# Decays of two chunks built by TensorE in PSUM ahead of block 0 of a fused SSD scan and MLP, and chunk 1's scan moved to the end of block 0

## Chip, cores, metric

One core of one Trainium2 chip. The metric is the time of one execution on the device in microseconds (us), the median of several runs; lower is better. The span of a profile is some 1.7 us shorter than the time of the same run (411.6 against 413.28 for the kernel before).

## The reference

A Mamba-2 style scan over 4 batches, 8 heads, 768 steps in chunks, then an MLP with hard-swish. Cut to what matters:

```python
log_a = np.log(np.clip(a, 1e-06, 1.0))          # a: (4, 8, 768)
for c in range(nc):
    cum = np.cumsum(la, axis=-1)
    L = np.exp(cum[:, :, :, None] - cum[:, :, None, :]) * causal     # the decays
    M = np.einsum('bhin,bhjn->bhij', Cc, Bc) * L
    y[:, :, sl] = M @ xc + (Cc @ state) * np.exp(cum)
    state = exp(sum(la)) * state + sum(B x * exp(cum[-1] - cum))
x = y.transpose(0, 2, 1, 3).reshape(3072, 256)
h = x @ w_in;  g = h * np.clip(h + 3.0, 0.0, 6.0) / 6.0;  out = g @ w_out   # w_in, w_out in float64
```

The kernel works on chunks of 128 steps. All 4 batches of one chunk (512 tokens) form one block of the MLP, so there are six blocks. The weights come as 64-bit floats and are decoded on the chip in eight parts, four of w_in and four of w_out, while block 0 runs.

## The kernel before

The decays of a chunk come by DMA: the cumulative sum is written to DRAM and read back, spread over all 128 partitions. GpSimd masks the upper triangle, and ScalarE takes the exp of one head at a time, with minus the sum at step j as its bias.

```python
nc.sync.dma_start(out=cum_d.rearrange("c g p -> g c p"), in_=cum)

def load_decay(c, b):
    L = big([P, NH, P], "L")
    src = cum_d[c, b * NH:(b + 1) * NH].rearrange("h p -> (h p)").unsqueeze(0)
    nc.sync.dma_start(out=L.rearrange("j h i -> j (h i)"), in_=src.to_broadcast([P, NH * P]))
    Ls[c, b] = L

def hide(c, b):                       # GpSimd, 128x1024
    nc.gpsimd.affine_select(out=L, in_=L, pattern=[[0, NH], [1, P]], compare_op=ALU.is_ge,
                            fill=-1e5, base=0, channel_multiplier=-1)
def decay(c, b):                      # ScalarE, 128x128 each
    for h in range(NH):
        nc.scalar.activation(L[:, h], L[:, h], AF.Exp, bias=cum_n[:, c, g:g + 1])
```

`turn` transposes B and C of two batches on TensorE, `scores` forms C B' of one batch on TensorE and multiplies it into L on VectorE, `mix` multiplies by x on TensorE, `keep` copies y and the state out. A decode of one weight part goes back and forth between ScalarE and VectorE:

```python
def decode(i):                                     # five stages, one per `yield`
    nc.scalar.copy(out=s, in_=top); yield
    e = s & 0x7FF0; s = s & 0x8000; yield          # VectorE
    nc.scalar.activation(e..., AF.Relu, ...); nc.scalar.activation(e, ..., AF.Relu, ...)
    m = hi & 0xFFFFF | 0x100000; yield             # VectorE
    m = lo * 2**-32 + m; e = e | s; load_w(i + NRAW); yield
    dst = m * 2**-20 * e                           # VectorE, writes w_in or w_out
```

The order of block 0, cut: the prologue runs chunk 0's scan; the first half (`mlp_in`) has chunk 1's exps and transposes between its columns; the second half (`mlp_out`) has chunk 1's scan beside the first batches.

```python
for f in range(NF):
    mlp_in(0, f); ...decode stages...; beside_in(1, f)    # exps, turn of chunk 1
beside_out(1, 0)
for i in range(NP):
    for b in range(2):
        mlp_out(0, b, i * FP, (i + 1) * FP)               # needs w_out part i
    ...decode stages of w_out...
    beside_out(1, i + 1)                                  # scores, mix, keep of chunk 1
mlp_out(0, 2, 0, NF); beside_out(1, 4); mlp_out(0, 3, 0, NF)
```

## Time and profile before

| | before |
|---|---|
| time, median (range) of 3 runs | 411.64 us (410.7 to 414.11) |
| block 0's first product h (end of the prologue) | 31.4 us |
| last part of w_in and first of w_out ready (end of the first half) | 67.7 us |
| block 1's first product h (end of the second half) | 112.2 us |
| from there to the end of the span | 299.4 us |

Read it as four stages: the first three are limited by different things, and the last is TensorE without a hole. The prediction shows the lines for this.

### The profile page before, as it was taken

How to read it: one execution, taken by the hardware profiler on the slowest of the kernel's cores; microseconds unless marked ns; L12 is line 12 of the kernel's file. 1: busy time of each engine (PE TensorE's matmuls, PEld its weight loads, DVE VectorE, ACT ScalarE, POOL GpSimd, SP SyncE). 2: the span in 40 equal slices, each digit the busy share in tenths (PEclk: the TensorE clock that was granted, in tenths of full speed). 3: DMA queues.
4: the chain of work that ended last, by engine and by line, in shares of the span. 5: the costliest groups of instructions: out<-in, count | busy, mean ns of one | idle time of the engine just before them, and what ended most of it. 6: DMA issues, size and time to landing. Idle time of an engine off the chain costs nothing.

```text
span 411.6 us, 6492 instructions
## 1 busy us (share of the span) xinstructions
PE 378.7 (92%) x2588; PEld 261.3 (63%) x2588; DVE 227.3 (55%) x414; ACT 163.0 (40%) x365; POOL 40.4 (10%) x42
## 2 busy tenths in 40 slices
PE   0487798759999999999999999999999999999995
PEld 0353344548844698844698844698744789744995
DVE  5367787990448864138854238844238834257611
ACT  5386899520179300079200188200188200133100
POOL 1326100060006000005000004000000000000000
PEclk9999989998999999999999999999999999999999
DMA  9897966940096000097000096000000000000000
GB/s 158 236 337 245 150 249 128 161 146 25 14 118 229 2 1 27 3 119 237 0 2 27 21 125 216 0 2 27 27 0 0 2 2 28 26 0 0 2 27 25
DMA packets 87614, 32.33 MB, mean 79 GB/s; under 512 B 75584, under 2 KB 81408, under 8 KB 87584
## 3 DMA queue, kind: packets, MB, share of 16 engines
q1 hardware_dynamic: 87584, 31.92, 37.3%
q8 instruction: 20, 0.33, 0.3%
q14 instruction: 10, 0.08, 0.1%
HBM read 28.67 MB, written 3.24 MB: 78 GB/s over the span
## 4 chain that ended last, share of the span: by engine, by line
PE 74%; DMA 9%; ACT 5%; issue 4%; DVE 4%; SPq 1%; POOL 1%; POOLq 0%; DVEq 0%; ACTq 0%
PE h L377 29%; PE ob L450 18%; PE oa L450 13%; PE o L391 6%; DMA L<-cum_d 5%; ACT L L250 3%; PE cb L304 3%; DMA bc<-in_C_dram 2%; PE y L336 2%; PE y L327 1%; DVE gT L383 1%; DMA eto<-cum_d 1%; ACT r L382 1%; POOL L L241 1%; SPq L202 1%
## 5 line engine op out<-in xcount | busy, mean ns | idle before, releaser
L377 PE MATMUL h<-yT,w_in 128*128 128x512 f32 x384 | 169.9, 598 | 4.7 <-DVE w_in L181 3.8
L377 PEld LDWEIGHTS h<-yT,w_in 128*128 128x128 f32 x384 | 72.2, 192 | 91.1 <-issue 78.8
L383 DVE SCALAR_TENSOR_TENSOR gT<-r,h 128x512 f32<-128x512 f32 x96 | 64.3, 683 | 61.6 <-ACT r L382 61.2
L382 ACT ACTIVATE r<-h,half 128x512 f32<-128x512 f32 x96 | 64.5, 685 | 73.4 <-PE h L377 70.3
L250 ACT ACTIVATE L<-L,cum_n 128x128 f32<-128x128 f32 x192 | 58.4, 397 | 4.5 <-POOL L L241 4.5
L312 DVE TENSOR_TENSOR L<-L,cb 128x256 f32<-128x256 f32 x96 | 33.8, 414 | 28.6 <-PE cb L304 28.6
L450 PE MATMUL ob<-t,gT 128*128 128x128 f32 x320 | 39.8, 278 | 0.0
L359 ACT COPY yT<-y 128x256 f32<-128x256 f32 x24 | 7.7, 374 | 80.5 <-PE y L344 61.7
L450 PEld LDWEIGHTS oa<-w_out,gT 128*128 128x128 f32 x320 | 37.2, 192 | 3.7 <-issue 3.7
L450 PEld LDWEIGHTS ob<-t,gT 128*128 128x128 f32 x320 | 37.3, 192 | 2.7 <-issue 2.7
L241 POOL TENSOR_SCALAR_AFFINE_SELECT L<-L 128x1024 f32<-128x1024 f32 x24 | 31.2, 1309 | 78.7 <-DMA L<-cum_d 67.6
L450 PE MATMUL oa<-w_out,gT 128*128 128x128 f32 x320 | 38.4, 276 | 0.0
L450 PE MATMUL ob<-w_out,s 128*128 128x128 f32 x320 | 38.2, 278 | 0.0
L450 PEld LDWEIGHTS ob<-w_out,s 128*128 128x128 f32 x320 | 36.5, 192 | 1.8 <-issue 1.5
L391 PE MATMUL o<-w_out,gT 128*128 128x256 f32 x128 | 30.6, 399 | 6.7 <-DVE w_out L181 6.7
L391 PEld LDWEIGHTS o<-w_out,gT 128*128 128x128 f32 x128 | 25.1, 199 | 11.8 <-DVE w_out L181 7.5
L304 PE MATMUL cb<-cT,bT 32*128 32x256 f32 x192 | 22.6, 472 | 6.5 <-DVE cT L285 5.4
L481 DVE TENSOR_TENSOR u<-ob,res 128x256 f32<-128x256 f32 x10 | 4.2, 425 | 30.6 <-PE ob L450 30.6
L450 PE MATMUL oa<-t,s 128*128 128x128 f32 x160 | 19.5, 275 | 0.0
L450 PEld LDWEIGHTS oa<-t,s 128*128 128x128 f32 x160 | 18.7, 192 | 0.0
L304 PEld LDWEIGHTS cb<-cT,bT 32*128 32x128 f32 x192 | 10.5, 203 | 12.6 <-DVE cT L285 6.5
L471 DVE TENSOR_TENSOR res<-oa,x 128x256 f32<-128x256 f32 x10 | 4.2, 425 | 24.4 <-PE oa L450 15.8
(64 smaller groups left out, 248.8 us busy)
## 6 DMA issues: line engine op xcount, KB each, us to landing
L<-cum_d SPq DMA_DIRECT2D x24, 512.0 KB, 6.9
raw<-in_moe_w_in_dram SPq DMA_DIRECT2D x4, 1024.0 KB, 8.3
raw<-in_moe_w_out_dram SPq DMA_DIRECT2D x4, 1024.0 KB, 6.8
xt<-in_x_dram SPq DMA_DIRECT2D x6, 512.0 KB, 8.7
out_dram<-res SPq DMA_DIRECT2D x20, 128.0 KB, 1.8
bc<-in_C_dram SPq DMA_DIRECT2D x6, 256.0 KB, 5.1
bc<-in_B_dram SPq DMA_DIRECT2D x6, 256.0 KB, 7.6
eto<-cum_d SPq DMA_DIRECT2D x40, 32.0 KB, 5.9
```

The lines of the kernel that those rows point to most:

```text
L241: nc.gpsimd.affine_select(out=L, in_=L, pattern=[[0, NH], [1, P]], compare_op=ALU.is_ge, fill=-1e5, base=0, channel_multiplier=-1)
L250: nc.scalar.activation(L[:, h], L[:, h], AF.Exp, bias=cum_n[:, c, g:g + 1])
L304: nc.tensor.matmul(out=cb.rearrange("j h i -> j (h i)"), lhsT=bT[rows, b % 2], rhs=cT[rows, b % 2].rearrange("n t i -> n (t i)"), start=Tr ...
L312: nc.vector.tensor_tensor(out=L[:, hs], in0=L[:, hs], in1=cbs[q], op=ALU.mult)
L336: nc.tensor.matmul(out=y_ps[u][32 * q:32 * q + 32, b % 2], lhsT=xt[:, b * NH + h], rhs=L[:, h], start=(c == 0), stop=True, tile_position=( ...
L359: nc.scalar.copy(out=yTs[c][:, u, bs_], in_=y_ps[u][:, 0:2])
L377: nc.tensor.matmul(out=h, lhsT=w_in[:, j, f * P:(f + 1) * P], rhs=yTs[k][:, j].rearrange("p b i -> p (b i)"), start=(j == 0), stop=(j == N ...
L382: nc.scalar.activation(r, h, AF.Relu, bias=half, scale=1.0 / 6.0)
L383: nc.vector.scalar_tensor_tensor(out=gTs[k][:, f], in0=r, scalar=1.0, in1=h, op0=ALU.min, op1=ALU.mult)
L391: nc.tensor.matmul(out=o, lhsT=gTs[k][:, f, b * P:(b + 1) * P], rhs=w_out[:, f], start=(f == 0), stop=(f == NF - 1))
L450: nc.tensor.matmul(out=bank[:, slot], lhsT=lhs[:, j], rhs=rhs[:, j], start=(j == 0), stop=(j == NJ - 1), skip_group_check=True)
L471: nc.vector.tensor_tensor(out=res[:, 0:5:4], in0=oa[:, 1:3], in1=x1[:, t:t + 1].to_broadcast([P, 2, P]), op=ALU.add)
```

## The change

Intent: spare chunks 0 and 1 the trip of their decays through DRAM, and take chunk 1's scan away from the weight decode. The differences cum_i - cum_j come from a product with 64 rows of contraction (32 rows carry cum_i, 32 carry -cum_j, and selecting vectors pick the batch and the head), added in PSUM onto a mask of 0 and -1e5 that a bf16 product with the identity has put there. ScalarE then takes the exp of 128x512 at once. All of it lies ahead of block 0. Chunk 1's scan moves to the last two batches of block 0's second half. The core of the diff, with cuts:

```diff
+    def diff_mask(c, b, u):
+        nc.tensor.matmul(
+            out=d, lhsT=ident_h, rhs=hide.unsqueeze(1).to_broadcast([P, HU, P]),
+            start=True, stop=True)
+    def diff_add(c, b, u):                       # 64 rows of contraction
+        nc.tensor.matmul(
+            out=ds[c, b, u], lhsT=d_lhs[:, b], rhs=d_rhs[:, HU * u:HU * u + HU],
+            start=False, stop=True, skip_group_check=True)
+    def diff_exp(c, b, u):
+        nc.scalar.activation(Ls[c, b][:, HU * u:HU * u + HU], ds.pop((c, b, u)), AF.Exp)
 ...
-    for b in range(NB):
-        hide(0, b)
+    for b in range(NB):
+        for u in range(2):
+            diff_mask(0, b, u)
+    ... log, scan, spread ...
+    for b in range(NB):
+        for u in range(2):
+            diff_add(0, b, u)
 ...
     scores(0, 0)
     scores(0, 1)
+    diff(1, 0, 0)                # mask, add, exp
+    diff(1, 0, 1)
     mix(0, (0,))
+    diff(1, 1, 0)
     scores(0, 2)
+    diff(1, 1, 1)
     mix(0, (1,))
 ...  (four more of chunk 1 among the rest)
         if k == 0:
-            beside_out(c, 0)
             for i in range(NP):
                 ... mlp_out(0, b, i * FP, (i + 1) * FP), decode of w_out ...
-                    beside_out(c, i + 1)
-            mlp_out(k, 2, 0, NF)
-            beside_out(c, 4)
+                if i + 2 == NP:
+                    ... from_start(1), carry(1), ends(1, b), turn(1, 0), turn(1, 1)
+            beside_out(1, 0)
+            mlp_out(0, 2, 0, NF // 2)
+            beside_out(1, 1)
+            ... and so on to beside_out(1, 4)
```

Smaller parts: `ends` uses the last column of L and not a separate exp; chunk 0's x is loaded earlier; one of four weight sums moves.

More of the change, by code (lines that the diff above doesn't have):

```diff
@@ L14 @@
 ALU = mybir.AluOpType
+AX = mybir.AxisListType
 PSUM = bass.MemoryType.PSUM
@@ L67 @@
     ctx.enter_context(tc.manual_schedule())
-    def big(shape, name):
-        return att.tile(shape, FP32, name=name, tag="big", bufs=8)
+    pre = ffn.tile([P, NF, TB], FP32, name="pre", tag="gT")
+    G = NB * NH
     moe_w_in, moe_w_out = moe_w_in.bitcast(U32), moe_w_out.bitcast(U32)
-    a_sb = big([NB * NH, S], "a_sb")
-    nc.sync.dma_start(out=a_sb, in_=a.rearrange("b h s -> (b h) s"))
+    a_sb = pre[:2 * G, 0:2].rearrange("g t i -> g (t i)")[:, :S]
+    for r in range(2):
+        nc.sync.dma_start(out=a_sb[r * G:(r + 1) * G], in_=a.rearrange("b h s -> (b h) s"))
     loaded = {}
@@ L115 @@
     load_bc(0)
+    load_x(0)
     nc.scalar.preload_act_table_set("natural_log_exp_and_others")
@@ L120 @@
     make_identity(nc, ident)
-    run = big([NB * NH, NC, P], "run")
+    ident_h = const.tile([P, P], BF16, name="ident_h")
+    hide = const.tile([P, P], BF16, name="hide")
+    nc.gpsimd.memset(hide, 0.0)
+    nc.gpsimd.affine_select(
+        out=hide, in_=hide, pattern=[[1, P]], compare_op=ALU.is_ge, fill=-1e5, base=0,
+        channel_multiplier=-1)
+    run = pre[:2 * G, 2:4].rearrange("g t i -> g (t i)")[:, :S]
+    run = run.rearrange("g (c p) -> g c p", p=P)
     nc.vector.memset(run, 1.0)
     nc.vector.memset(run[:, :, 0:1], 0.0)
+    nc.vector.tensor_copy(ident_h, ident)
     half = const.tile([P, 1], FP32, name="half")
@@ L139 @@
     nc.vector.tensor_reduce(
-        out=parity, in_=head.rearrange("p q t -> p t q"), axis=mybir.AxisListType.X,
+        out=parity, in_=head.rearrange("p q t -> p t q"), axis=AX.X,
         op=ALU.add)
@@ L182, in decode @@
             out=dst, in0=m, scalar=2.0 ** -20, in1=e, op0=ALU.mult, op1=ALU.mult)
-    cum = big([NB * NH, NC, P], "cum")
-    rest = big([NB * NH, NC, P], "rest")
-    flat = cum.rearrange("g c p -> g (c p)")
-    nc.vector.tensor_scalar(
-        out=a_sb, in0=a_sb, scalar1=1e-6, scalar2=1.0, op0=ALU.max, op1=ALU.min)
-    nc.scalar.activation(a_sb, a_sb, AF.Ln)
-    nc.vector.tensor_tensor_scan(
-        out=flat, data0=run.rearrange("g c p -> g (c p)"), data1=a_sb, initial=0.0,
-        op0=ALU.mult, op1=ALU.add)
@@ L194 @@
-    cum_d = dram.tile([NC, NB * NH, P], FP32, name="cum_d")
-    nc.sync.dma_start(out=cum_d.rearrange("c g p -> g c p"), in_=cum)
+    one_h = const.tile([2 * G, NH], FP32, name="one_h")
+    one_b = const.tile([2 * G, NB], FP32, name="one_b")
+    eye = ident[:2 * G, :2 * G]
+    nc.vector.tensor_reduce(
+        out=one_h, in_=eye.rearrange("g (x h) -> g h x", h=NH), axis=AX.X, op=ALU.add)
+    nc.vector.tensor_reduce(
+        out=one_b, in_=eye.rearrange("g (r b h) -> g b r h", r=2, h=NH), axis=AX.XY, op=ALU.add)
@@ new lines @@
+    nc.vector.tensor_scalar(
+        out=one_b[G:], in0=one_b[G:], scalar1=-1.0, scalar2=None, op0=ALU.mult)
+    d_lhs = pre[:2 * G, 6].rearrange("g (b j) -> g b j", b=NB)
+    d_rhs = pre[:2 * G, 7:9].rearrange("g t (h i) -> g (t h) i", i=P)
+    nc.vector.tensor_copy(d_lhs[:G], one_b[:G].unsqueeze(2).to_broadcast([G, NB, P]))
+    nc.gpsimd.tensor_copy(d_rhs[G:], one_h[G:].unsqueeze(2).to_broadcast([G, NH, P]))
+    cum = pre[:2 * G, 4:6].rearrange("g t i -> g (t i)")[:, :S]
+    cum_c = cum.rearrange("g (c p) -> g c p", p=P)
@@ new lines, with log_a, add_up, spread @@
+    ends_at = (slice(0, P), slice(P, S))
+    def log_a(sl):
+        nc.vector.tensor_scalar(
+            out=a_sb[:, sl], in0=a_sb[:, sl], scalar1=1e-6, scalar2=1.0, op0=ALU.max, op1=ALU.min)
+        nc.scalar.activation(a_sb[:, sl], a_sb[:, sl], AF.Ln)
+    def add_up(sl):
+        nc.vector.tensor_tensor_scan(
+            out=cum[:, sl], data0=run.rearrange("g c p -> g (c p)")[:, sl], data1=a_sb[:, sl],
+            initial=0.0, op0=ALU.mult, op1=ALU.add)
+    def spread(engine, c):
+        engine.tensor_tensor(
+            out=d_lhs[G:], in0=cum_c[G:, c:c + 1].to_broadcast([G, NB, P]),
+            in1=one_b[G:].unsqueeze(2).to_broadcast([G, NB, P]), op=ALU.mult)
+        for u in range(2):
+            hs = slice(HU * u, HU * u + HU)
+            engine.tensor_tensor(
+                out=d_rhs[:G, hs], in0=cum_c[:G, c:c + 1].to_broadcast([G, HU, P]),
+                in1=one_h[:G, hs].unsqueeze(2).to_broadcast([G, HU, P]), op=ALU.mult)
@@ L197 @@
+    cum_d = dram.tile([NC, G, P], FP32, name="cum_d")
     Ls, etos = {}, {}
     def load_decay(c, b):
-        L = big([P, NH, P], "L")
+        Ls[c, b] = L = att.tile([P, NH, P], FP32, name="L", bufs=2 * NB)
         src = cum_d[c, b * NH:(b + 1) * NH].rearrange("h p -> (h p)").unsqueeze(0)
@@ L203, in load_decay @@
             out=L.rearrange("j h i -> j (h i)"), in_=src.to_broadcast([P, NH * P]))
-        Ls[c, b] = L
     def load_eto(c):
@@ L212, in load_eto, with conceal @@
         etos[c] = eto
-    for b in range(NB):
-        load_decay(0, b)
-    load_x(0)
-    load_w(1)
-    load_w(2)
-    cum_n = const.tile([P, NC, NB * NH], FP32, name="cum_n")
-    e_from = const.tile([P, NC, NB * NH], FP32, name="e_from")
-    def by_token():
-        nc.vector.tensor_tensor(
-            out=rest, in0=cum[:, :, P - 1:P].to_broadcast([NB * NH, NC, P]), in1=cum,
-            op=ALU.subtract)
-        c_ps = ps.tile([P, 2, NC, NB * NH], FP32, name="c_ps", tag="f")
-        for k, src in enumerate((cum, rest)):
-            for c in range(NC):
-                nc.tensor.transpose(
-                    out=c_ps[:, k, c], in_=src[:, c], identity=ident[:NB * NH, :NB * NH])
+    cum_n = const.tile([P, NC, G], FP32, name="cum_n")
+    def by_token():
+        c_ps = ps_o.tile([P, NC, G], FP32, name="c_ps", tag="o")
+        for c in range(2, NC):
+            nc.tensor.transpose(out=c_ps[:, c], in_=cum_c[:G, c], identity=ident[:G, :G])
         nc.vector.tensor_scalar(
-            out=cum_n, in0=c_ps[:, 0], scalar1=-1.0, scalar2=None, op0=ALU.mult)
-        nc.scalar.activation(e_from, c_ps[:, 1], AF.Exp)
+            out=cum_n[:, 2:], in0=c_ps[:, 2:], scalar1=-1.0, scalar2=None, op0=ALU.mult)
     yTs, states, bTs, bss, tmps, y_pss, CBs = {}, {}, {}, {}, {}, {}, {}
-    def hide(c, b):
+    ds = {}
+    def diff_mask(c, b, u):
+        k = 2 * b + u
+        if c == 0 and k < 4:
+            d = ps.tile([P, HU, P], FP32, name="d", tag="f")
+        elif c == 0 and k >= 6:
+            d = ps_y.tile([P, HU, P], FP32, name="d", tag=f"y{u}")
+        else:
+            d = ps_o.tile([P, HU, P], FP32, name="d", tag="o")
+        nc.tensor.matmul(
+            out=d, lhsT=ident_h, rhs=hide.unsqueeze(1).to_broadcast([P, HU, P]),
+            start=True, stop=True)
+        ds[c, b, u] = d
+    def diff_add(c, b, u):
[3 more added lines that the diff above has]
+    def diff_exp(c, b, u):
+        if u == 0:
+            Ls[c, b] = att.tile([P, NH, P], FP32, name="L", bufs=2 * NB)
+        nc.scalar.activation(Ls[c, b][:, HU * u:HU * u + HU], ds.pop((c, b, u)), AF.Exp)
+    def conceal(c, b):
         L = Ls[c, b]
@@ L253, in from_start, with ends, carry @@
         nc.scalar.activation(etos[c], etos[c], AF.Exp)
-    def ends(c):
-        bc, xt = loaded[c]
+    def ends(c, b):
         if c < NC - 1:
-            bs = att.tile([P, NB * NH, N], FP32, name="bs")
+            if b == 0:
+                bss[c] = att.tile([P, G, N], FP32, name="bs")
+            hs = slice(b * NH, b * NH + NH)
             nc.gpsimd.tensor_tensor(
-                out=bs, in0=bc[:, 1],
-                in1=e_from[:, c].unsqueeze(2).to_broadcast([P, NB * NH, N]), op=ALU.mult)
-            bss[c] = bs
-        if 0 < c < NC - 1:
-            tmp = att.tile([P, NB, 2 * D], FP32, name="tmp", bufs=1)
+                out=bss[c][:, hs], in0=loaded[c][0][:, 1, hs],
+                in1=Ls[c, b][:, :, P - 1:P].to_broadcast([P, NH, N]), op=ALU.mult)
+    def carry(c):
+        if c < NC - 1:
+            tmps[c] = att.tile([P, NB, 2 * D], FP32, name="tmp", bufs=1)
             nc.gpsimd.tensor_tensor(
-                out=tmp, in0=states[c - 1],
+                out=tmps[c], in0=states[c - 1],
                 in1=etos[c][:, :, P - 1:P].to_broadcast([P, NB, 2 * D]), op=ALU.mult)
-            tmps[c] = tmp
     def turn(c, p):
         bc, xt = loaded[c]
-        t_ps = ps_o.tile([P, 4, P], FP32, name="t_ps", tag="o")
+        pool, tag = (ps, "f") if c < 2 else (ps_o, "o")
+        t_ps = pool.tile([P, 4, P], FP32, name="t_ps", tag=tag)
         for k in range(4):
@@ L299, in scores @@
             rows = slice(32 * q, 32 * q + 32)
-            if c == 0 and b % 2 and q < 2:
-                cb = ps_o.tile([P, 2, P], FP32, name="cb", tag="o")
-            else:
-                cb = ps.tile([P, 2, P], FP32, name="cb", tag="f")
+            cb = ps.tile([P, 2, P], FP32, name="cb", tag="f")
             nc.tensor.matmul(
@@ L318, in mix @@
         if bs[0] % 2 == 0:
-            y_pss[c] = [ps_y.tile([P, 4, P], FP32, name=f"y{u}") for u in range(NK)]
+            y_pss[c] = [ps_y.tile([P, 4, P], FP32, name=f"y{u}", tag=f"y{u}") for u in range(NK)]
         y_ps = y_pss[c]
@@ L411, in weight_sums @@
         t2, t4 = (att.tile([P, NJ, P], FP32, name=n, tag="wm") for n in ("t2", "t4"))
-        for o, p_, q_, op in ((t3, w4[:, 1, 1], w4[:, 0, 1], ALU.subtract),
+        t1 = w4[:, 0, 1]
+        wsums.update({1: t1, 2: t2, 3: t3, 4: t4})
+        for o, p_, q_, op in ((t3, w4[:, 1, 1], t1, ALU.subtract),
                               (t2, t3, w4[:, 0, 0], ALU.add),
-                              (t4, w4[:, 1, 0], t2, ALU.subtract)):
+                              (t4, w4[:, 1, 0], t2, ALU.subtract),
+                              (t1, t1, w4[:, 0, 0], ALU.subtract)):
             nc.vector.tensor_tensor(out=o, in0=p_, in1=q_, op=op)
-        wsums.update({1: w4[:, 0, 1], 2: t2, 3: t3, 4: t4})
-    def weight_sum_in_place():
-        nc.vector.tensor_tensor(
-            out=w4[:, 0, 1], in0=w4[:, 0, 1], in1=w4[:, 0, 0], op=ALU.subtract)
+            yield
     gsums = {}
@@ L492, in beside_in, with rows @@
     def beside_in(c, f):
-        if c > 1 and f < 2:
-            hide(c, 2 * f)
-            hide(c, 2 * f + 1)
+        if f < 2:
+            conceal(c, 2 * f)
+            conceal(c, 2 * f + 1)
         if f == 3:
             from_start(c)
-        if f == 4:
-            ends(c)
-        if f in ((4, 8, 12, 15) if c == 1 else (2, 4, 6, 8)):
-            decay(c, (f - 1) // 4 if c == 1 else f // 2 - 1)
+            carry(c)
+        if f in (2, 4, 6, 8):
+            decay(c, f // 2 - 1)
+            ends(c, f // 2 - 1)
         if f in (7, 11):
             turn(c, f // 8)
+    def rows(c):
+        for b in range(NB):
+            load_decay(c, b)
+        load_eto(c)
     def beside_out(c, b):
-        if b == 0 and c + 1 < NC:
-            for i in range(NB):
-                load_decay(c + 1, i)
-            load_eto(c + 1)
         if b in (2, 4):
@@ L528, in weights, with diff, decay_first @@
             next(parts[i], None)
+    def diff(c, b, u):
+        diff_mask(c, b, u)
+        diff_add(c, b, u)
+        diff_exp(c, b, u)
     for b in range(NB):
-        hide(0, b)
-    weights(0, 3)
-    by_token()
+        for u in range(2):
+            diff_mask(0, b, u)
+    for sl in ends_at:
+        log_a(sl)
+    add_up(ends_at[0])
+    spread(nc.vector, 0)
+    for b in range(NB):
+        for u in range(2):
+            diff_add(0, b, u)
     weights(0, 2)
-    turn(0, 0)
-    for b in range(NB):
-        load_decay(1, b)
+    add_up(ends_at[1])
+    nc.sync.dma_start(out=cum_d[1:].rearrange("c g p -> g c p"), in_=cum_c[:G, 1:])
+    load_w(1)
+    load_w(2)
     load_eto(1)
     load(1)
-    decay(0, 0)
+    def decay_first(b):
+        for u in range(2):
+            diff_exp(0, b, u)
+        ends(0, b)
+    decay_first(0)
+    weights(0, 1)
+    decay_first(1)
+    spread(nc.gpsimd, 1)
+    decay_first(2)
+    weights(0, 1)
+    turn(0, 0)
     turn(0, 1)
-    ends(0)
-    decay(0, 1)
+    decay_first(3)
     scores(0, 0)
-    decay(0, 2)
     scores(0, 1)
+    diff(1, 0, 0)
+    diff(1, 0, 1)
     mix(0, (0,))
-    decay(0, 3)
-    for b in range(NB):
-        hide(1, b)
+    diff(1, 1, 0)
     scores(0, 2)
+    diff(1, 1, 1)
     mix(0, (1,))
     keep(0, 0)
-    weights(1, 1)
+    diff(1, 2, 0)
+    diff(1, 2, 1)
     scores(0, 3)
     mix(0, (2,))
-    weights(1, 1)
+    weights(0, 1)
+    diff(1, 3, 0)
+    diff(1, 3, 1)
     mix(0, (3,))
@@ L561 @@
     weights(1, 1)
-    weave = {0: [1], 1: [1]}
+    by_token()
+    weave = {0: [1, 1], 1: [1], 2: [1]}
     for i in range(2, NP + 1):
@@ L578 @@
                     weights(i, 1)
-            if c < NC:
+            if k and c < NC:
                 beside_in(c, f)
             if k:
-                if k == 1 and f == 1:
-                    weight_sum_in_place()
+                if k == 1 and f in (1, 3):
+                    next(sums)
                 for j0 in SUMS.get(f, ()):
@@ L593 @@
                     weights(NP + i + 1, 2)
-                    if i + 2 < NP:
-                        weights(NP + i + 2, 3)
-                    beside_out(c, i + 1)
-            mlp_out(k, 2, 0, NF)
-            beside_out(c, 4)
-            weight_sums()
-            mlp_out(k, 3, 0, NF)
+                if i + 2 < NP:
+                    weights(NP + i + 2, 3)
+                if i + 2 == NP:
+                    from_start(1)
+                    carry(1)
+                    for b in range(NB):
+                        ends(1, b)
+                    turn(1, 0)
+                    turn(1, 1)
+            rows(2)
+            sums = weight_sums()
+            beside_out(1, 0)
+            mlp_out(0, 2, 0, NF // 2)
+            beside_out(1, 1)
+            next(sums)
+            mlp_out(0, 2, NF // 2, NF)
+            beside_out(1, 2)
+            next(sums)
+            mlp_out(0, 3, 0, NF // 2)
+            beside_out(1, 3)
+            mlp_out(0, 3, NF // 2, NF - FP)
+            beside_out(1, 4)
+            mlp_out(0, 3, NF - FP, NF)
         else:
@@ L603 @@
                 if c < NC and i in SCAN:
+                    if i == 1 and c + 1 < NC:
+                        rows(c + 1)
                     beside_out(c, SCAN[i])
```

## The prediction

The 17.3 us added on TensorE are 16 pairs of about 1.08, of which 0.86 is the difference (two records of 0.43, from the trace; 13.8 us for all sixteen) and the rest the mask. The 8.6 for chunk 1's eight pairs, and with it the 32.2, the 106.7 and the 406.2, hold it too.

> **What bounds the kernel now.** I first read the busy tenths in 40 slices (10.3 us each), then busy time by stage, then the chain of waits, then the instructions in order of time.
>
> ```profile
> PE   0487798759999999999999999999999999999995
> DVE  5367787990448864138854238844238834257611
> DMA  9897966940096000097000096000000000000000
> ```
>
> From slice 11 on TensorE is never idle; before that it has holes while the DMA and VectorE rows are high. So the end is set by TensorE from about 112 us, and what can be won lies in front of it. The table by stage says it in numbers (columns: stretch, its length, busy time and count of TensorE, weight loads, VectorE, ScalarE, GpSimd, then clock, DMA share, GB/s). I cut it where block 0's first matmul starts (31.4), where its output matmuls start (69.5), and where block 1 starts (112.0):
>
> ```profile
> 0.00:31.40 31.40, 14.69 (x148) 10.16 (x148) 16.69 (x38) 18.02 (x45) 6.58 (x14) 1.00 1.02 247
> 31.40:69.50 38.10, 33.24 (x80) 14.57 (x80) 30.60 (x43) 32.62 (x64) 8.29 (x6) 0.96 0.80 193
> 69.50:112.00 42.50, 35.79 (x281) 29.16 (x281) 25.64 (x41) 12.07 (x16) 6.76 (x5) 0.96 0.54 92
> 112.00:173.60 61.60, 61.22 (x459) 42.98 (x458) 34.05 (x62) 22.52 (x57) 6.84 (x6) 1.00 0.35 63
> 173.60:234.00 60.40, 60.40 (x457) 42.54 (x457) 33.27 (x64) 22.15 (x56) 6.54 (x6) 1.00 0.36 66
> ```
>
> Blocks 1 and 2 are TensorE through and through. Block 0 takes 80.6 us where a later one takes 60.4, although it also waits for weights that have to be decoded. Who makes TensorE wait there, from the waits between 31.4 and 112 us:
>
> ```profile
> PE o L391 <- DVE w_out L181: 6.7, 2, 4.4
> PE h L377 <- DVE w_in L181: 3.8, 2, 2.2
> ```
>
> It waits for the last step of a weight decode, on VectorE. In order of time, the decode of the last part beside chunk 1's scan and beside GpSimd's masking of chunk 2's decays:
>
> ```profile
> 80.65 1.23 DVE L181 SCALAR_TENSOR_TENSOR w_out<-wm,we 128x1024 f32<-128x1024 f32 x1
> ...
> 83.19 1.41 DVE L312 TENSOR_TENSOR L<-L,cb 128x256 f32<-128x256 f32 x4
> ...
> 85.47 2.11 DVE L168 SCALAR_TENSOR_TENSOR wm<-raw,wm 128x1024 f32<-128x1024 uint32 x1
> 87.50 1.57 DVE L170 TENSOR_TENSOR we<-we,ws 128x1024 uint16<-128x1024 uint16 x1
> 89.11 1.96 DVE L181 SCALAR_TENSOR_TENSOR w_out<-wm,we 128x1024 f32<-128x1024 f32 x1
> ```
>
> Two parts finish 8.5 us apart (81.9 and 91.1), 1.4 of it the scan's four multiplies, and 2.5 of it because the three last steps take 5.64 instead of the 3.14 that they take elsewhere. The prologue, by the same list: chunk 0's decay rows land only at 16.7 us (cumulative sum ready at 6.2, written to DRAM, read back to 128 partitions), then eight exps per batch, 0.305 apart, then scores and mix; block 0 starts at 31.4.
>
> [...]a 128x512 product is two records, paced 0.43 us (64 in 27.5 us). [...]the 1.22 us step above took 2.11 beside the masking, whereas the multiply with a PSUM input stayed at 1.41 for four. [...]Here 75,584 of 87,614 packets are under 512 B, and in the first two slices the engines are 0.9 busy at 158 and 236 GB/s.
>
> **The prologue after the change.** Removed: the round trip of chunk 0's and 1's decays through DRAM (8 transfers of 512 KB), eight masks on GpSimd (about 1.1 us each), 64 small exps (19.5 us of ScalarE). Added on TensorE: per half batch a bf16 mask product[...] and an fp32 difference with 64 rows (0.86: columns count, not rows), 16 of each: 17.3 us. Added on ScalarE: 16 exps of 128x512, taken at 0.6 to 0.69 as the relu of that shape, 10.5 us. Added on VectorE: three 32x512 products, 0.6 each by the 0.94 of the 32x768 subtraction.
>
> In order: a lands twice by 3.4; the constants keep VectorE until 3.7, the short slice is clamped, logged and scanned by 4.7, the three products end at 6.5. Differences run on TensorE from about 6 to 13. ScalarE's copy of the first raw weights (landing near 7) ends at 8.1, so chunk 0's exps lie between 8.1 and 16, with 2.3 us of decode relus among them. Turns 13.0 to 14.3, scores 0 at 14.6, and scores 1 can end only when VectorE has multiplied batch 0 (1.41 us): 16.6 to 17.2. From there TensorE's order is fixed and full: 8 difference pairs of 1.08 = 8.6, four mixes of about 1.1 (their pace now, 24.02 to 25.25) = 4.4, two scores of 0.7 = 1.4, together 14.4, to 31 or 31.6. Two copies of y follow, and block 0 starts at **32.2** against 31.4. So I give the prologue no gain: the DRAM wait is exchanged for 17 us of products, half of them for chunk 1.
>
> **Block 0's first half.** TensorE needs 27.5 us and has 38 now, so the decode's ring between VectorE and ScalarE counts. One part in steady state: first mask 0.42, ScalarE's two relus 2.3 and the next r 0.67, gT, then 1.14 + 0.6 + gT + 1.13 + gT on VectorE: 8.15 us per part (from 50.39 to 59.29 it is 8.9 now, because bT and csT stand in the ring, and 9.7 one part earlier, because ScalarE waits for eto). Part 1 has three stages left to do that lie in the prologue now: +1.2. Sum: 1.6 + 0.75 + 0.85 - 1.2 = 2.0 less; part 4 is ready 34.4 after the start (now 36.3), at **66.6** against 67.7.
>
> **Block 0's second half.** Now the four quarters of batches 0 and 1 start at 69.56, 76.21, 82.34, 91.12. Without the scan's multiplies and GpSimd's masks a part takes 0.42 + 2.3 + 0.65 + 1.15 = 4.6 us (the interval of 5.72 now less 1.41 is 4.3; the relus bind instead). Counted from 66.6: quarters at 0, 5.8, 10.4, 15.0, plus 0.5 if chunk 2's masks, whose rows come early, catch the last steps; each quarter is 3.6 of TensorE. End of the fourth: 19.1 later. Then TensorE alone: 64 records by 0.224 = 14.3, scores 4 by 0.64 = 2.6, two double mixes by 1.83 = 3.7, a wait of 0.4 for the last multiply: 21.0. VectorE has 5.6 of multiplies and 2.4 of weight sums there and fits. Block 1 starts at 66.6 + 40.1 = **106.7** instead of 112.0.
>
> **The rest.** Blocks 1 to 5 keep their TensorE work. One more weight sum (1.22) on VectorE in block 1, and four smaller GpSimd products for one, lie beside it: VectorE is busy 34 of 61.6 there. 411.6 - 5.3 gives 406.3; I say **406.2**.
>
> **Rivals.** *A: TensorE becomes the bound in the prologue more than I think.* For it: fixed order, only two spare banks for chunk 1's differences, and each mix and score waits for VectorE or ScalarE between. If every pair waits 0.5 more, block 0 starts at 36 and the time is 410. Against it: exps of 0.6 to 0.7 are shorter than a pair of 1.08. *B: DMA hides the gain.* x of chunk 0 now follows 8,192 packets of 64 B in the queue, may land at 18 to 19, just when the first mix wants it, and pushes everything else back; w_in parts come behind chunk 1's loads. If these bind, 2 to 4 us are lost: 408 to 410. Against: 4 MB of row transfers are gone from a queue that is full until 56 us. *C: the ring of the decode is looser than I count* when decays no longer share ScalarE: in the first half VectorE's own work is 6.65 per part, not 8.15. If the ring fell to 7.2, three parts give 3 us more, and with a prologue 2 us shorter the time is 401. Against: the program's order puts the relus ahead of the next r. *D: nothing moves, as TensorE only meets the same work later.* The second half has 36 us of products in 42.5, so it can give at most 6.5 and the first half 10; no hidden floor takes the whole gain.
>
> **Range and chances.** Start of block 0 is uncertain by 2 us, each half by 1.5: together about 3, and the model by hand a little more. Range **401.5 to 410.5**. Faster by over 2% means under 403.4: 0.25. Slower means over 419.9, a wait that I overlook: 0.03. Within 2%: 0.72.
>
> **What would show it.** Block 0's first h near 32, with TensorE busy without holes from 17 to 31 and differences paced 0.86; difference exps at 0.6 to 0.7; parts of w_in 8.2 apart; quarters of the output 4.6 apart with 1.2 us last steps; block 1 at 106.7; later blocks at 60.4. Wrong would be: a first h before 29 or after 35; TensorE waiting for x or a w_in part because of a DMA; w_out steps still stretched by GpSimd; or later blocks that change by over 0.5 us each.

## More of the kernel before

The instructions in order of time give for one batch's scores (start, busy time of the group, engine, line, operation, operands, count; first in the prologue, then in block 0's second half; PE is TensorE, PEld its weight load, DVE VectorE, ACT ScalarE):

```profile
27.64 0.52 PEld L304 LDWEIGHTS cb<-cT,bT 32*128 32x128 f32 x8 [0.17 <-issue]
27.64 1.24 PE L304 MATMUL cb<-cT,bT 32*128 32x256 f32 x8
...
73.21 0.31 PEld L304 LDWEIGHTS cb<-cT,bT 32*128 32x128 f32 x8 [0.33 <-DVE L L312]
73.21 0.71 PE L304 MATMUL cb<-cT,bT 32*128 32x256 f32 x8
```

The same eight products take 1.24 us at 27.6 and 0.71 at 73.2, and their weight loads 0.52 and 0.31. Idle time ahead of an instruction stands apart, in the brackets, so waiting does not explain the ratio: TensorE itself was slower.

## The result

434.44 us (median of 4 runs, 432.84 to 434.81) against 412.61 (4 runs of before in the same rounds): a ratio of 1.0524, 95% interval 1.0468 to 1.0581, so 5% slower. (Ratios here are the mean time of one kernel's fast runs over that of the other's of the same rounds, so not quite the ratio of the medians.) The prediction was 406.2 with a range to 410.5, and gave "slower" 3 chances in 100.

The profile after by stage, cut at block 0's first h, at the end of the last w_in and first w_out decode, and at block 1's first h, where the last line ends (columns as in the prediction):

```profile
0.00:55.24 55.24, 51.54 (x188) 20.56 (x188) 19.05 (x44) 16.67 (x28) 7.27 (x19) 1.00 0.73 124
55.24:92.50 37.26, 31.68 (x65) 13.15 (x64) 26.42 (x41) 23.82 (x30) 0.00 (x0) 0.95 0.25 90
92.50:132.70 40.20, 37.97 (x296) 30.34 (x297) 26.82 (x47) 13.46 (x19) 8.20 (x9) 0.96 0.62 117
```

The whole loss is in the first line: the prologue takes 55.2 us where 31.4 were needed, TensorE is busy for 51.5 of it, and the other engines for less than 20. The chain of work that ended last, between 0 and 60 us (start, us, what):

```profile
6.96 13.99 PE d L284 x16
...
27.19 0.54 PE d L278
27.73 2.00 PE d L284 x2
29.73 0.54 PE d L278
30.27 2.00 PE d L284 x2
```

Sixteen records of differences (two per fp32 product) take 13.99 us, 0.86 to 0.87 each, where 0.43 was expected, and each later mask and difference takes 2.54 and not 1.08. The pace is not one of these instructions only. When block 0 starts, h, which has 128 full rows, has it too, and then loses it (weight loads of h, in order of time):

```profile
57.11 0.34 PEld L430 LDWEIGHTS h<-yT,w_in 128*128 128x128 f32 x1 [0.52 <-issue]
57.97 0.34 PEld L430 LDWEIGHTS h<-yT,w_in 128*128 128x128 f32 x1 [0.52 <-issue]
...
59.21 0.19 PEld L430 LDWEIGHTS h<-yT,w_in 128*128 128x128 f32 x1 [0.24 <-issue]
```

From 55.2 to 58.7 the records start 0.86 apart and a weight load takes 0.34; from 58.8 on they are 0.43 and 0.19. TensorE had run at half its pace from the start to 58.7 us. The table by stage nevertheless prints a granted clock (the share of its full clock that TensorE is allowed) of 1.00 for the first stage. That column cannot be used here: the clock's record in this trace begins at 58.7 us, with the first fast records, and what lies before it is counted as 1.00 (a weight load takes 0.33 us there). In what follows the clock is released when the pace of such a record of 512 columns goes from 0.86 us to 0.43, and lost when it goes back.

It was released 3.5 us into h (55.2 to 58.7). But the differences had kept TensorE busy without a gap for 14 us (6.96 to 20.89) and released nothing. Why not was the question for the experiments.

By stage, from the profiles (us):

| | before | predicted | after |
|---|---|---|---|
| first h of block 0 | 31.4 | 32.2 | 55.2 |
| first half | 36.3 | 34.4 | 37.3 |
| second half | 44.5 | 40.1 | 40.2 |
| block 1 to the end | 299.4 | 299.6 | 300.4 |

### The profile page after: what moved, and what is told of

It reads as the page before. It is cut to its first block, busy times and chain, and to the rows that moved or that the text cites. A ratio compares the mean times of both kernels' runs of the same rounds, so it can differ in the third digit from the quotient of the medians.

```text
span 433.1 us, 6522 instructions
## 1 busy us (share of the span) xinstructions
PE 416.5 (96%) x2628; PEld 271.1 (63%) x2628; DVE 232.2 (54%) x423; ACT 154.3 (36%) x317; POOL 38.1 (9%) x55
## 4 chain that ended last, share of the span: by engine, by line
PE 74%; ACT 12%; DVE 10%; issue 1%; DMA 1%; POOL 0%; SPq 0%; ACTq 0%; DVEq 0%; POOLq 0%
PE h L430 19%; PE ob L503 17%; PE oa L503 13%; PE d L284 7%; PE o L444 6%; ACT L L304 6%; PE cb L357 4%; ACT r L435 3%; PE y L389 3%; DVE gT L436 3%; DVE s L490 2%; PE y L380 1%; DMA bc<-in_C_dram 1%; ACT we L174 1%; ACT we L173 1%
## 5 line engine op out<-in xcount | busy, mean ns | idle before, releaser
L430 PE MATMUL h<-yT,w_in 128*128 128x512 f32 x384 | 172.0, 604 | 5.7 <-DVE w_in L192 4.7
L304 ACT ACTIVATE L<-L,cum_n 128x128 f32<-128x128 f32 x128 | 39.1, 398 | 0.0
L503 PEld LDWEIGHTS ob<-t,gT 128*128 128x128 f32 x320 | 37.3, 192 | 2.7 <-issue 2.7
L444 PE MATMUL o<-w_out,gT 128*128 128x256 f32 x128 | 31.5, 401 | 3.1 <-DVE w_out L192 3.1
L284 PE MATMUL d<-pre 64*128 64x512 f32 x32 | 30.6, 1102 | 1.3 <-DVE pre L233 1.3
L295 POOL TENSOR_SCALAR_AFFINE_SELECT L<-L 128x1024 f32<-128x1024 f32 x16 | 20.9, 1338 | 9.4 <-DMA L<-cum_d 8.8
L315 POOL TENSOR_TENSOR bs<-bc,L 128x128 f32<-128x128 f32 x20 | 9.2, 468 | 142.2 <-issue 88.1
L357 PE MATMUL cb<-cT,bT 32*128 32x256 f32 x192 | 20.8, 473 | 0.3 <-DVE cT L341 0.3
L291 ACT ACTIVATE L<-d 128x512 f32<-128x512 f32 x16 | 9.4, 597 | 28.0 <-PE d L284 27.9
```

What stands on the lines that cost most here:

```text
L284: nc.tensor.matmul(out=ds[c, b, u], lhsT=d_lhs[:, b], rhs=d_rhs[:, HU * u:HU * u + HU], start=False, stop=True, skip_group_check=True)
L291: nc.scalar.activation(Ls[c, b][:, HU * u:HU * u + HU], ds.pop((c, b, u)), AF.Exp)
L357: nc.tensor.matmul(out=cb.rearrange("j h i -> j (h i)"), lhsT=bT[rows, b % 2], rhs=cT[rows, b % 2].rearrange("n t i -> n (t i)"), start=Tr ...
L430: nc.tensor.matmul(out=h, lhsT=w_in[:, j, f * P:(f + 1) * P], rhs=yTs[k][:, j].rearrange("p b i -> p (b i)"), start=(j == 0), stop=(j == N ...
L444: nc.tensor.matmul(out=o, lhsT=gTs[k][:, f, b * P:(b + 1) * P], rhs=w_out[:, f], start=(f == 0), stop=(f == NF - 1))
L503: nc.tensor.matmul(out=bank[:, slot], lhsT=lhs[:, j], rhs=rhs[:, j], start=(j == 0), stop=(j == NJ - 1), skip_group_check=True)
```

## The experiments

Theories at the outset. **R (rows)**: products that fill 64 of 128 rows do not count as work that releases the clock. **D (data)**: the operands are nearly all zero, and that is why. **A (adding)**: an fp32 product added onto a bank costs this by itself, at any clock.

### pad128: the same product with 128 rows

```diff
+    nc.gpsimd.memset(pre[2 * G:, 6:9], 0.0)
-            out=ds[c, b, u], lhsT=d_lhs[:, b], rhs=d_rhs[:, HU * u:HU * u + HU],
+            out=ds[c, b, u], lhsT=d_lhs_all[:, b], rhs=d_rhs_all[:, HU * u:HU * u + HU],   # 128 partitions
```

> The changed kernel with the difference products padded to 128 rows (rows 64 to 127 of both operands zero), nothing else. Theory R (rows: TensorE stays at half its pace through the prologue because products that fill 64 of 128 rows do not count as work that releases the clock): the difference stream starts near 7 us at 0.86 per record, goes over to 0.43 between 10 and 14 us, block 0's first h comes at 32 to 37 us instead of 55, time 411 to 418. Theory D (data: operands that are nearly all zero do not release it): zeros are added, so nothing moves, 434. Theory A (adding onto a bank at this pace is what an fp32 product with start=False costs): nothing moves, 434.

413.2 us (4 runs, 412.49 to 413.87), ratio to before 1.0002 (0.9935 to 1.007); correct. In order of time on TensorE:

```profile
7.64 10.05 PE L287 MATMUL d<-pre 128*128 128x512 f32 x16 [1.97 <-DVE pre L236]
...
22.44 1.02 PE L287 MATMUL d<-pre 128*128 128x512 f32 x2
```

Sixteen records take 10.05 us and not 13.99: slow at first, then fast. A later pair of two records takes 1.02 and not 2.07, and block 0 starts at 35.9. Rows of zeros that add nothing to the result and nothing to the data win 21 us. R expected this; D and A expected nothing and fall as explanations of it.

### dense64 and dense64b: 64 rows, no zeros

```diff
+    nc.vector.memset(one_h, 0.1)
+    nc.vector.memset(one_b, 0.1)
```

> Wrong result on purpose: the selecting vectors one_h and one_b are set to the constant 0.1, so the two operands of the 64-row difference products have no zero columns or rows; instructions and shapes are those of the changed kernel. Theory R: nothing moves, first h at 54 to 56, 432 to 437 us. Theory D: the clock is released within the first 14 us of differences, first h at 32 to 37, 411 to 418. Theory A: nothing moves.

431.6 us in one run (wrong result). The clock came back at 48.9 us in it (the expectation below says 48.4), before block 0, which no theory had said, so it was timed:

> dense64 once more, timed (wrong result on purpose). In its one look the 14 us stream of 64-row differences was as slow as in the changed kernel, but the clock came back at 48.4 us, among mixes, scores and differences, instead of at 58, and the time was 431.6. If dense operands help in that mixed part (a weak form of theory D), its runs lie at 428 to 432 and the profile shows the return before block 0 again.[...]

429.83 us (4 runs: 433.82, 431.57, 428.09, 426.61; the first is slow). The three fast runs have a ratio to before of 1.0376 (1.0303 to 1.0449), slower, where the changed kernel had 1.0524 (1.0468 to 1.0581). In the profile, which fell on the slow run, the stream is as it was in the changed kernel, and the clock came back only at 59.3 us, in block 0:

```profile
6.95 13.99 PE L286 MATMUL d<-pre 64*128 64x512 f32 x16 [1.29 <-DVE pre L235]
```

Dense operands did not release the clock in the stream. Four runs lie 1 to 6 us below every run of the changed kernel (lowest 432.84), so the operands may have a part later on, among scores and mixes; by the fast runs it is some 6 of the 21 us. No profile of a fast run of dense64b exists, and this stays open. A rival is chance in when the clock is released (the expectation's sentence on it, with 430 to 435 us, is cut). The three fast runs have mean granted clocks of 0.944 to 0.952 and the slow one 0.999. Without dense operands, too, the fastest run of the changed kernel (432.84) has 0.937 where its other three have 0.992. In the profiles of before and of the changed kernel the clock's record begins with the first release (at 30.4 and 58.7 us), and slow time ahead of it does not lower the mean, so these three and that one probably had an early release that was lost again. No trace of them exists.

### warm64: release the clock first

```diff
+    for _ in range(2):                    # the eight masks of chunk 0 twice more
+        ... nc.tensor.matmul(out=ds[0, b, u], lhsT=ident_h, rhs=hide..., start=True, stop=True)
```

> The changed kernel with the eight bf16 mask products of chunk 0 sent three times (24 in a row from about 2 us, full rows, ending near 9 to 12 instead of 5.5). Theory R: the masks go from 0.43 to 0.22 between 5.5 and 9 us; the first differences run at 0.43 a record and fall back to 0.86[...]; the later 64-row pairs are slow again; time 428 to 438. Theory D: the masks are nearly all zeros too (an identity against zeros and -1e5) and stay at 0.43; everything shifts later by 3 to 5 us, 436 to 440. Theory A: masks go to 0.22, the first difference is 0.86 at once.

Four runs: 414.53 (the profiled one), 428.67, 426.15, 426.24 (these three slow, for being over 1.5% above the fastest). The profiled one:

```profile
5.45 4.08 PE L596 MATMUL d<-hide,ident_h 128*128 128x512 bf16 x16
9.47 7.13 PE L284 MATMUL d<-pre 64*128 64x512 f32 x16
```

The masks released the clock, although they too are nearly all zeros (against D), and 64-row differences then ran at 0.43 (against A). But they did not fall back as I had expected under R: all 16 stayed fast, and so did the rest of this run. The three other runs are 12 to 14 us slower with a mean granted clock of 0.96. Either 64-row products hold the clock for a while and then lose it, or they hold it always and something else loses it.

### hold64: does a 64-row stream keep a released clock?

On top of the edit of warm64:

```diff
+    for _ in range(4):                     # 64 records of 64-row differences, then fresh masks
+        ... nc.tensor.matmul(out=ds[0, b, u], lhsT=d_lhs[:, b], rhs=..., start=True, stop=True)
```

> Clock released by 24 full-row bf16 masks as in warm64, then 64 extra records of 64-row differences in a row (dummies, overwritten by fresh masks), then the kernel as changed. Question: does a 64-row stream only fail to release the clock, or does it also lose it? If it keeps it (as the profiled run of warm64, where all differences stayed at 0.43), 64 records take 27.5 us at 0.43 and the time is 412 to 416 plus 29, 441 to 446. If it loses it (my reading of the three other runs of warm64, 426 to 429 at a mean granted clock of 0.96), records go from 0.43 to 0.86[...] and stay there, 470 to 490 us.

458.26 us, one run, between the two expectations, because both happened one after the other:

```profile
39.21 7.13 PE L284 MATMUL d<-pre 64*128 64x512 f32 x16
...
48.12 2.96 PE L357 MATMUL cb<-cT,bT 32*128 32x256 f32 x16 [0.75 <-DVE cT L341]
51.33 2.07 PE L284 MATMUL d<-pre 64*128 64x512 f32 x2
53.34 0.61 PE L278 MATMUL d<-hide,ident_h 128*128 128x512 bf16 x1
```

From 9.7 to 46.3 us a stream of 64-row products, with only one group of masks in it, ran at 0.43 a record. So 64 rows held a released clock, for 36 us here. It was lost at 51.3. The only pause since 9.7 is one of 0.75 us ahead of the scores, which ran from 48.12 on for 2.96 us and whose products have 32 rows. In warm64's profile the same scores after the same pause did not lose it (18.37, 2.96 us; the next difference pair takes 1.12); in pad96 below it is lost right after them. From there mixes, scores, masks and 64-row differences in alternation, with no gap, did not bring it back before block 0. The table by stage agrees; here its clock column does work, as there had been a release before:

```profile
9.70:46.30 36.60, 36.60 (x90) 15.54 (x89) 3.17 (x4) 5.32 (x8) 0.82 (x2) 1.00 0.85 142
51.00:79.00 28.00, 28.00 (x142) 10.38 (x141) 5.02 (x13) 5.94 (x12) 0.00 (x0) 0.50 0.00 1
```

Theory R thus gets its final form, as far as these runs go: a stream of 64-row differences did not release the clock in 14.0 us (the changed kernel, dense64, dense64b), but once released it was kept through 36 us of such a stream (hold64). That the lost clock is the scores' doing, by their 32 rows, is argued and not shown. That warm64's slow runs lost it in the same place is likely from their clock of 0.96 (an estimate: 0.04 of 425 us are 17 us lost, so 34 us at half pace, and the same sum gives 37 for hold64: 0.041 of 456.5 us, doubled), but no trace of such a run exists.

### pad96: where is the bound?

```diff
+    nc.gpsimd.memset(pre[2 * G:3 * G, 6:9], 0.0)      # 96 rows, not 128
```

> As pad128, but with zero rows 64 to 95 only, so the differences fill 96 of 128 rows. Theory R with a bound between 64 and 96 rows: as pad128, first h near 36, 411 to 415. With a bound above 96: slow as the changed kernel, first h near 55, 431 to 436. No theory of mine says which.

411.4 us, one run; correct.

```profile
7.64 7.11 PE L287 MATMUL d<-pre 96*128 96x512 f32 x16 [1.97 <-DVE pre L236]
```

The differences are fast from the first on, but 96 rows did not bring the first release: it came after chunk 0's eight masks (2.1 to 5.7), which are still slow (3.60 us for eight), and before the first difference at 7.6. TensorE had run nothing but these masks, so they released it, which the same masks did not do in the profiled run of the changed kernel; it differed between these runs. What speaks for 96 rows comes later. The clock went away at 19.8 and came back at 23.2, and in between TensorE ran 96-row differences and one mask; with 64 rows such a stretch had not brought it back (hold64). This is one run, and a stream of 96 rows alone was not tested.

### warmpad: both

> Both together: masks three times and differences padded to 128 rows. Theory R: masks go to 0.22, differences at 0.43 from the first on, ending at 15 to 18 us; first h at 31 to 35, time 408 to 414, so about the kernel before or 1% faster. Theories D and A: 434 to 440, differences at 0.86.

415.51 us (4 runs, 411.72 to 416.68), ratio 1.0047 (0.9971 to 1.0123). The edit is that of pad128 and warm64 together. In the profiled run (the fastest) differences take 7.03 us from the first on and block 0 starts at 33.8, as expected; block 1 starts at 109.6. But two of the others are 5 us slower at a mean granted clock of 0.979, and the median misses the expectation. Two more rounds of masks are no gain over pad128 in the median.

### duo: two 64-row products at once

This version and the two after it contain the extra masks of warm64. The operands are kept on both halves of the partitions, and the two half batches use one half each (`tile_position`), into two banks.

```diff
-    for r in range(2):                                  # a loaded twice
+    for r in range(4):
-            lhsT=d_lhs[:, b], rhs=d_rhs[:, HU * u:HU * u + HU], start=False, ...
+            lhsT=d_lhs[2 * G * u:2 * G * u + 2 * G, b], rhs=d_rhs[2 * G * u:2 * G * u + 2 * G],
+            tile_position=(2 * G * u, 0), start=False, ...
```

> Masks three times, and the differences of the two half batches on rows 0 to 63 and 64 to 127 at the same time (operands kept on both row halves, two banks), so both halves of the array work. If two 64-row products side by side count as a full array and really overlap, a pair of differences takes 0.9 to 1.0 instead of 1.75, and of 13.8 us of differences 6 go: first h at 28 to 30, block 1 near 104 to 106, time 404 to 409. If they do not overlap: as warmpad, 410 to 415.[...]

411.97 us (4 runs, 411.15 to 412.32), ratio 0.997 (0.995 to 0.9991); correct.

```profile
9.60 3.70 PE L289 MATMUL d<-pre 64*128 64x512 f32 x16
...
17.04 4.01 PE L362 MATMUL cb<-cT,bT 32*128 32x256 f32 x16 [2.71 <-DVE cT L346]
```

They overlap fully: 3.70 us and not 7.13. The gain then vanished in the next line: the scores wait 2.71 us for VectorE, the clock is lost from 16.9 to 23.7 (4.01 us for sixteen, against 2.96 in warm64), and block 0 starts at 33.8, as in warmpad. The expected 404 to 409 was missed.

### duodefer: chunk 1's differences inside block 0's first half

```diff
-    diff(1, 0) ... diff(1, 3)                           # out of the prologue
+                if f in (1, 4, 8, 12):                  # into mlp_in of block 0
+                    diff(1, f // 4)
```

(The operands get a buffer of their own, as block 0's results overwrite the old one.)

> As duo, with chunk 1's four pairs of differences moved from the prologue into block 0's first half, where TensorE waits for w_in anyway. First h at 24 to 27; the first half 35.5 to 38 long instead of 35.5 because 8 exps join ScalarE; block 1 at 100 to 104; time 400 to 406, faster than both kernels by 1.5 to 3%. If the exps lengthen the decode ring by their full 4.8 us, block 1 near 106 and 406 to 409.

408.35 us (4 runs, 407.98 to 409.72), ratio 0.9891 (0.9862 to 0.992); correct. The lowest median, 1.1% below the kernel before: clear of noise, but within the 2% that count as the same. The expected 400 to 406 was missed; the time lies in the range for exps that lengthen the decode ring, and the first h came at 28.4 and not at 24 to 27. By stage (the second line ends where the output products start):

```profile
0.00:28.44 28.44, 23.66 (x181) 13.40 (x181) 18.64 (x48) 11.25 (x20) 5.95 (x17) 0.78 0.90 189
28.44:65.80 37.36, 34.99 (x89) 14.05 (x89) 27.21 (x41) 26.91 (x36) 0.00 (x0) 0.99 0.48 138
```

Block 0 starts 3 us earlier than before and block 1 5.3 us earlier. The clock is lost again at 15.8 us (mean 0.78 of the prologue) and comes back at 29.4, 1 us after block 0's start. (The expectation of duohot says 17 and 32, which misreads the trace: h's weight loads are at 0.19 from 29.4 on.)

### duohot: keep the clock with dummies

```diff
+    hot(12)             # bf16 masks into a spare bank; 2 or 3 more between scores and mixes
     scores(0, 0)
```

> duodefer with 21 dummy bf16 full-row masks into a spare bank, in the places of chunk 0's scan where TensorE waits for VectorE (12 before the first scores, 2 or 3 between scores and mixes). In duodefer the clock was lost near 17 us and came back only at 32 (scores 1.24 instead of 0.71, first h at 0.86 a record). If the dummies hold it: scores at 0.71, first h at 25 to 26.5 instead of 28.4 and its first records at 0.43, block 1 near 103, time 404 to 406 against 408.4. If dummies only take TensorE's time: 408 to 411.

409.29 us (6 runs, 408.7 to 410.19), ratio 0.9916 (0.9878 to 0.9954); correct. The hoped-for 404 to 406 was missed, and the time is that of the other branch, in which dummies only take TensorE's time. The clock held (scores 0.71, granted 0.996), but block 0 started at 28.8 and not at 25 to 26.5: between 15.9 and 28.8 the dummies themselves take 5.4 us of TensorE. Nor would an earlier start have helped much, as far as these two traces show. Block 0's later columns wait for the same decode of w_in whether TensorE is fast or not. In both kernels they start at the same time (first duodefer, then duohot):

```profile
40.09 1.98 PE L436 MATMUL h<-yT,w_in 128*128 128x512 f32 x4 [2.37 <-DVE w_in L192]
```

```profile
40.05 1.98 PE L436 MATMUL h<-yT,w_in 128*128 128x512 f32 x4 [2.39 <-DVE w_in L192]
```

Once chunk 1's differences are out of the prologue, a clock kept by dummies wins nothing: they use up what they win, and the decode of w_in binds next. What the prologue would do at full clock without dummies is not shown.

## Why the prediction was wrong

**The step that failed.** "Added on TensorE: per half batch a bf16 mask product [...] and an fp32 difference with 64 rows (0.86: columns count, not rows), 16 of each: 17.3 us." The 0.86 was taken from block 0, at full clock, and both were put where the pace is still half of that. Measured: 0.43 for a mask and 1.71 for a difference where they stand in rows of their own kind (chunk 0), and 2.54 for the two where they alternate (chunk 1). In the prologue's sum this makes: differences of chunk 0 end at 20.9 and not 13.0 (7 of the 7.9 us by their pace); turns and scores up to chunk 1's first mask 6.2 us and not 3.9; from there to block 0's start 28.1 and not 15.3, of which eight pairs at 2.54 for 1.08 make 11.7. Together 7.9 + 2.3 + 12.8 = 23.0, which is 55.2 less 32.2.

"Columns count, not rows" is right for the duration at a given clock: 64, 96 and 128 rows all take 0.43 (sixteen records in 7.13 us in warm64, 7.11 in pad96 and 7.03 in warmpad). It is wrong for what the product does to the clock. In pad128 differences of 128 rows released it at 13.6 us, in pad96 differences of 96 rows with one mask among them between 19.8 and 23.2, and 64 rows did not in 14.0 us of the changed kernel; in hold64 64 rows kept it for 36 us.

**What I had overlooked.** Rival A asked if TensorE would bind the prologue and put its worst case at 410, from waits. The pace itself was on no list. The trace of before had it: scores at 1.24 us in the prologue and 0.71 later. The prediction's sum for the prologue took scores at the fast 0.7 and mixes at the slow 1.1 side by side, without asking why. A clock column of 1.00 seemed to exclude it. The prediction did name a first h after 35 as a sign of being wrong, and it came at 55.2.

**The prologue at full pace.** With the row fault mended, block 0 starts at 35.9 (pad128) and 33.8 (warmpad's profiled run) against the 32.2 predicted. The rest of the gap is the slow time until the release, and differences that start at 7.6 to 8.6 and not at 6. The statement that the prologue would give nothing was right: it trades a wait for DMA for TensorE's work, and it comes out 2.4 to 4.5 us behind the kernel before. duodefer shows the way out: half of that work was not needed there.

**Block 0's first half**: 34.4 predicted, 37.3 measured, 35.6 in pad128 and in warmpad. Some 1.7 us of the difference came with the slow start of h in the changed kernel; most of the other 1.2 is the decode ring, 8.6 per part (67.77 to 76.40, 76.40 to 84.96) and not 8.15.

**Block 0's second half**: 40.1 predicted, 40.2 measured (in pad128 and warmpad 40.2, too). This mechanism was right in its parts. TensorE starts the fourth quarter of batches 0 and 1 at 108.1, 15.6 after the first (15.0 to 15.5 predicted, 21.6 before). The decode steps that took longer beside GpSimd's masks are short again, all but the last (VectorE, in order of time):

```profile
104.52 1.22 DVE L179 SCALAR_TENSOR_TENSOR wm<-raw,wm 128x1024 f32<-128x1024 uint32 x1
105.81 0.69 DVE L181 TENSOR_TENSOR we<-we,ws 128x1024 uint16<-128x1024 uint16 x1
106.54 1.54 DVE L192 SCALAR_TENSOR_TENSOR w_out<-wm,we 128x1024 f32<-128x1024 f32 x1
```

They are 3.45 us together, against 5.64 before. That the last one is still long was partly luck for the sum: the 0.5 us that the prediction kept for chunk 2's masks came true, but those masks came at 118.1 and this step ran beside GpSimd's products of `ends` (107.0 to 109.5). One reading in the prediction is wrong and did not matter: the two parts finished 9.2 us apart (81.9 to 91.1), not 8.5. The waits of TensorE in block 0, which were 6.7 us for w_out and 3.8 for w_in, are now (total, number, longest):

```profile
PE h L430 <- DVE w_in L192: 4.7, 2, 3.8
PE o L444 <- DVE w_out L192: 3.1, 2, 2.2
```

So the second half gained its 4.3 us (44.5 to 40.2), and the prologue's 23.8 buried it. No run separates the moved scan from the masks that GpSimd no longer runs there.

**The rest** keeps its time within 1 us (300.4 against 299.4). **Rival B**, the DMA, did not show: TensorE waits for no transfer in the prologue, nor in that of pad128, which runs at full clock from 13.6 us on. The sum 23.0 + 2.9 + 0.1 + 0.8 = 26.8 us is the span of 433.1 less the predicted 106.7 + 299.6. The 1.4 that are left to the 28.2 between the times come from the 406.2, which was worked out from a span and compared with times.

## What to carry to other kernels

Before a TensorE duration is used for a stage, look at that stage's own weight loads or at the same instruction there; here the ratio of about two between two stages was the clock, whatever the clock column said (1.00 for the first 55 us of the changed kernel, and 0.50 in hold64 for the same pace after a release). Products like these, added to a prologue, should either have 128 rows (which released the clock in pad128, at 13.6 us; 96, with a mask between, did in one run) or not stand on the path, since a stream with 64 rows released the clock in no profiled run here, in 14 us. And where a later stage has idle TensorE time beside a decode, new products belong there: chunk 1's differences, which took 20 us of the changed kernel's prologue (8 by 2.54), made block 0's first half 1.8 us longer in duodefer than in warmpad (37.4 against 35.6, up to the first output product), there with two half batches at once.
